# Decay tables ahead of the third piece of w_out, and the fifth tile's scores, mask and exit in another place

## The chip, the cores and the metric

The kernel runs on one core of a Trainium2 chip. The metric is the device time of one execution in microseconds (us); the figures given for the kernel before are a median of three runs. The profile is one further execution, recorded instruction by instruction. TensorE does the matrix products, VectorE and ScalarE the elementwise work and the copies out of PSUM, GpSimd a little elementwise work and the issue of nearly all loads, and SyncE issues stores and the transposing DMAs.

## The reference, cut to what matters

```
# q, k, v: (4 batches, 8 heads, 768 positions, 64), f32
state = gamma[h] * state + k_t (outer) v_t        # gamma[h] = 1 - 2**(-5-h)
y_t   = q_t @ state / sqrt(64)                    # for each of 768 positions
x = y, heads side by side                         # (3072 tokens, 512)
h = x @ w_in                                      # w_in: 512 x 2048
g = h + sin(alpha*h)**2 / (alpha + 1e-9)
out = g @ w_out                                   # w_out: 2048 x 512, out f32
```

## The kernel before

The recurrence is computed in chunks of 128 positions. A tile is one chunk of one batch with all eight heads, and there are 24 tiles. `order` (also `P`) puts the first chunks of the four batches in front, `P[0]` to `P[3]`, which need no state; then come chunks 1 to 5 of batch 0, `P[4]` to `P[8]`, then those of the other batches. The "fifth tile" is `P[4]`, the "sixth" is `P[5]`.

Each tile's q and k are transposed ("turned": `stage_T` on TensorE with a copy out of PSUM, or `turn`, a transposing DMA from SyncE), scores are formed in PSUM tile `pa` (`scores`), multiplied by a 0/1 mask on VectorE (the "mask" step, L349), and the values, scaled by `scale_v` (L156), are summed with them. `burst(old, new)` issues on TensorE what is left of tile `old`, with the scores of tile `new` in between, and returns four closures to be run later. These are `keep` (new state into `s_f`, L446), `hand` (its bf16 copy `s_q`, L452), `mask` (of tile `new`), and `exit` (`leave`, L433 or L436: the tile's result times the decay table `qg[:, c]` goes to `xT`, the input of the second part). With `apart=True` the result lies in two separate PSUM banks and the exit is two instructions. `decay_table(c)` (L229) makes the table for chunk index c on GpSimd, one 128x512 f32 product; five are made.

The second part is the two products with w_in and w_out. `Slot` computes 128 of the 2048 hidden columns for a group of tiles: matmuls L481, the sine on ScalarE L484, the square on ScalarE (L489) or on VectorE (L491, two inputs in SBUF), and the sum on VectorE (`add`, L496), which writes `gT` and frees the slot's PSUM bank. `ff_out` (L506) multiplies `gT` with w_out into `po`. Group 0 has four tiles, the other ten have two each. `F(ts, fs)` issues the w_out products of group 0's tiles `ts` for columns `fs`. When it reaches column 15 it also copies the result out (`take`: L520 on ScalarE for tile 0, L518 on VectorE for tile 1) and SyncE stores it. `fill(n)` issues the next n of the remaining w_out products of tiles 2 and 3. What is left of them after the bursts goes to `phase(1)`. Phases 1 to 10 are alike: slots of one group between products of the group before and a burst at two places.

Every queue is in program order: the schedule is written out by hand, each engine executes its instructions as they are issued in the text and waits at each for its inputs and its buffer. PSUM tags: `mm` has four banks, `pa` and `two` one tile of two banks each. In `two` lie in turn group 0's first two results (`both`) and the `py` of each burst from the sixth tile on.

GpSimd issues the loads in the order of the text: four pieces each of w_in and w_out, in between the first q, k, v tiles. `load_w_in(i, h)` loads columns 4i to 4i+3 in two halves, `load_w_out(i)` the rows for columns 4i to 4i+3 ("third piece" is i = 2). Slot f needs piece f // 4 of w_in, and the product of column f needs piece f // 4 of w_out. GpSimd also scales v of the fifth tile (`scale_v(P[4], nc.gpsimd)`), VectorE that of the sixth.

Of the kernel before, what the change touches and what calls it, by code (L numbers as in the profile page):

```python
# [16 lines left out]
def kernel(  # L17
# [15 lines left out]
    nc = tc.nc  # L33
    B, H, S, D = q.shape
    C = 128
    NCH = S // C
# [33 lines left out]
    def half(x):  # L70
        return slice(64 * x, 64 * x + 64)
# [6 lines left out]
    def spread(j):  # L78

        return j in order[8:11]  # L80

    def chunk_of(t, j):
        b, c = divmod(j, NCH)
        return t[b, :, c * C:(c + 1) * C, :].rearrange("h s d -> s h d")

    def load_chunk(j, names="qkv"):
        for name, src in (("q", q), ("k", k), ("v", v)):
            if name not in names:
                continue
            if name == "v":  # L90
                t = big.tile([128, H, D], BF16, name="vr", tag="vr", bufs=11)
            else:
                if ("qk", j) not in raw:
                    raw["qk", j] = big.tile([128, 2, H, D], BF16, name="qkr", tag="qkr", bufs=9)
                t = raw["qk", j][:, "qk".index(name)]
            if name != "v" and spread(j):
                for o in range(2):
                    nc.gpsimd.dma_start(out=t[:, NP * o:NP * o + NP], in_=chunk_of(src, j)[:, o::2])
            else:
                nc.gpsimd.dma_start(out=t, in_=chunk_of(src, j))  # L100
            raw[name, j] = t

    def wide(j):
        return j >= NCH + 3 and j % NCH > 0
# [24 lines left out]
    def load_w_in(i, h=None):  # L129
        c = slice(i * fw, (i + 1) * fw) if h is None else slice(i * fw + h * fw // 2, i * fw + (h + 1) * fw // 2)  # L130
        nc.gpsimd.dma_start(out=w_in[:, :, c], in_=w_in_v[:, :, c])

    def load_w_out(i, h=None):
        c = slice(i * fo, (i + 1) * fo) if h is None else slice(i * fo + h * fo // 2, i * fo + (h + 1) * fo // 2)
        nc.gpsimd.dma_start(out=w_out[:, c, :], in_=w_out_v[:, c, :])
# [16 lines left out]
    def scale_v(j, eng):  # L152
        t, by = raw["v", j], kg
        if wide(j):
            t, by = t.rearrange("i f p d -> i (f p) d"), kgq
        eng.tensor_mul(t, t, by[:, j % NCH, :, None].to_broadcast([128, H, D]))  # L156
# [71 lines left out]
    def decay_table(c):  # L228
        nc.gpsimd.tensor_mul(qg[:, c], qg[:, 0], step[:, c, :, None].to_broadcast([128, NP, C]))  # L229
# [27 lines left out]
    def stage_T(j, eng=None, tag="two"):  # L257
        pt = psum.tile([128, 2 * NP, 128], BF16, name="pt", tag=tag, bufs=4 if tag == "mm" else 1)
        st["qkT", j] = work.tile([128, 2 * NP, 128], BF16, name="qkT", tag="qkT", bufs=6)
        for i in range(2):  # L260
            for p in range(NP):
                for e in range(2):
                    h = 4 * (p % 2) + 2 * e + p // 2
                    nc.tensor.transpose(pt[half(e), i * NP + p, :], raw["qk"[i], j][:, h, :], ident)
        if eng is nc.scalar:
            nc.scalar.copy(st["qkT", j], pt)
        else:
            nc.vector.tensor_copy(st["qkT", j], pt)
# [70 lines left out]
    def scores(j):  # L339

        qkT = st["qkT", j]
        pa = st["pa", j] = psum.tile([128, 2, 512], F32, name="pa", tag="pa")
        if not wide(j):
            for p in range(NP):
                for f, e in tiles4:
                    nc.tensor.matmul(pa[half(f), e, 128 * p:128 * p + 128], qkT[half(e), NP + p, half(f)],  # L346
                                     qkT[half(e), p, :], start=(p == 0), stop=True, skip_group_check=True)
            aT = st["aT", j] = work.tile([128, 2, NP, 128], BF16, name="aT", tag="aT", bufs=2)
            return {"mask": lambda: nc.vector.tensor_mul(aT.rearrange("p e n t -> p (e n) t"),  # L349
                                                         pa.rearrange("p e (n t) -> p (e n) t", n=NP), mask_bc)}  # L350
        for m in range(2):
            for b, e in tiles4:
                nc.tensor.matmul(pa[half(b), e, 192 * m:192 * m + 128].rearrange("p (f i) -> p f i", f=2),
                                 qkT[half(e), 2 + m, half(b)], qkT[half(e), m:m + 5:4, half(b)],
                                 start=(m == 0), stop=True, skip_group_check=True)
            for b, e in tiles4:
                nc.tensor.matmul(pa[half(b), e, 192 * m + 128:192 * m + 192],
                                 qkT[half(e), 6 + m, half(b)], qkT[half(e), 4 + m, half(b)],
                                 start=False, stop=True, skip_group_check=True)
        aT = st["aT", j] = work.tile([128, 2, 2, 192], BF16, name="aTw", tag="aT", bufs=2)  # L360
        return {"mask": lambda: nc.vector.tensor_mul(aT, pa[:, :, 0:384].rearrange("p e (m t) -> p e m t", m=2),  # L361
                                                     maskq[:, None, None, :].to_broadcast([128, 2, 2, 192]))}
# [96 lines left out]
    def run(more, *kinds):  # L459
        for kind in kinds:  # L460
            if more and kind in more:
                more.pop(kind)()
# [40 lines left out]
    def ff_out(g, ts, f):  # L503
        if (g, ts) not in po:
            po[g, ts] = psum.tile([128, d_model], F32, name="po", tag="mm", bufs=4)
        nc.tensor.matmul(po[g, ts], gT[g][:, f, ts * C:(ts + 1) * C], w_out[:, f, :],  # L506
                         start=(f == 0), stop=(f == FF - 1))
        if f == FF - 1 and (g, ts) not in ((0, 0), (0, 1)):
            take(g, ts)

    def take(g, ts):
        o_sb = work.tile([128, d_model], F32, name="o_sb", tag="o_sb", bufs=3)
        if (g, ts) == end:
            h = d_model // 2
            nc.vector.tensor_copy(o_sb[:, :h], po[g, ts][:, :h])
            nc.scalar.copy(o_sb[:, h:], po[g, ts][:, h:])
        elif g > 0 or ts == 1:
            nc.vector.tensor_copy(o_sb, po[g, ts])  # L518
        else:
            nc.scalar.copy(o_sb, po[g, ts])  # L520
        nc.sync.dma_start(out=out_view[:, groups[g][ts], :], in_=o_sb)
# [75 lines left out]
        scale_v(j, nc.vector)  # L597
    for h in range(2):
        load_w_in(2, h)
    decay_table(1)  # L600
    decay_table(2)
    load_w_out(2)
    for h in range(2):
        load_w_in(3, h)
    decay_table(3)
    decay_table(4)
    load_chunk(order[4], "qk")
    load_w_out(3)
    decay_table(5)
    load_chunk(order[4], "v")  # L610
    for j in order[5:7]:
        load_chunk(j)
# [29 lines left out]
    P = order  # L642
    n3, n4 = 3 * C, 4 * C
    def F(ts, fs):
        for f in fs:
            for t in ts:
                ff_out(0, t, f)
        if FF - 1 in fs:
            for t in ts:
                take(0, t)  # L650

    def early(f, tag="mm"):
        return Slot(0, f, (0, n3), tag=tag)
# [3 lines left out]
    def fill(n):  # L657
        for _ in range(n):
            outs.pop(0)()

    fourth = psum.tile([128, 2, 512], BF16, name="fourth", tag="two", padded_shape=[128, 2, 1024])
    a = early(0).sq("A")
    b = early(1).sq("A")
    half_T(e3, 0, nc.vector, fourth[:, 0])
    c = early(2).sq("A")
# [14 lines left out]
    a = Slot(0, 0, (n3, n4), 4, "pa")  # L680
    F((0, 1, 2), (3,))
    a.sq("D").add()
    a = Slot(0, 4).sq("A")
    for f in range(5, FF):
# [6 lines left out]
        a = b  # L691
# [3 lines left out]
            first_state(e0)  # L695
        if f == 13:
            stage_T(P[4], nc.vector, "pa")
    F((0, 1), (13,))
    scale_v(P[4], nc.gpsimd)
    m4 = scores(P[4])["mask"]  # L700
    m4()
    fill(3)
    stage_T(P[5], nc.scalar, "mm")
    fill(1)
    a.add()
    scale_v(P[5], nc.vector)
    fresh = burst(P[4], P[5], apart=True)
    run(fresh, "keep", "hand", "mask", "exit")
    F((0, 1), (14,))
    F((0, 1), (15,))  # L710


    load_chunk(P[7])
# [3 lines left out]
    load_chunk(P[8], "v")  # L717
    scale_v(P[7], nc.gpsimd)
    load_chunk(P[10], "qk")
    load_chunk(P[9], "v")  # L720
    scale_v(P[8], nc.gpsimd)
    load_chunk(P[10], "v")
# [83 lines left out]
```

## Time and profile before

| | |
|---|---|
| time, median of 3 runs | 212.26 us (212.02 to 212.61) |
| time of the profiled execution | 212.17 us |
| its span, first to last instruction | 210.3 us |
| TensorE busy | 202.7 us (96%) |
| VectorE busy | 156.6 us (74%) |
| ScalarE busy | 154.9 us (74%) |
| GpSimd busy | 117.2 us (56%) |
| granted TensorE clock | 0.998 |

The profiled execution's own time is 1.87 us more than its span: what lies before the first and after the last instruction. A timeline row gives start, duration, engine, source line, operation, output and input tiles, and count; a bracket at its end gives the time that the engine sat idle before the row and what ended that. A duration is from start to end, and consecutive rows of one engine may overlap by some hundredths, as pipelined instructions do.

### The profile page before, as it was taken

The numbers are of one execution on the slowest core, as the hardware profiler recorded it, in microseconds if no ns is written. First come the engines' busy times: TensorE is split into PE (matmuls) and PEld (weight loads), VectorE is DVE, ScalarE is ACT, GpSimd is POOL, SyncE is SP. The second block draws the span as 40 slices with busy tenths as digits, with TensorE's granted clock in tenths as the row PEclk, the third lists the DMA queues.
The fourth block names the chain that finished last, engine by engine and source line by source line (L and its number), as shares of the span: only waits on it lengthen the run. The fifth ranks groups of instructions, "written<-read, shape, count | busy, mean of one in ns | idle before, by whom it ended". The sixth has DMA issues, their size and how long they took to land.

```text
span 210.3 us, 5890 instructions
## 1 busy us (share of the span) xinstructions
PE 202.7 (96%) x2418; PEld 129.9 (62%) x2418; DVE 156.6 (74%) x326; ACT 154.9 (74%) x325; POOL 117.2 (56%) x157
## 2 busy tenths in 40 slices
PE   7899889999999999999999999999999999999994
PEld 3445434456777666666666666766666766666653
DVE  5788998877888987777777777767768768666540
ACT  7778767556998877877777787786786787788821
POOL 8999976799989999998399901002022020000000
PEclk9999999999999999999999999999999999999999
DMA  9999999999999999999999996412412110110112
GB/s 130 152 177 198 201 198 183 154 162 172 155 123 169 121 178 165 170 119 169 177 83 180 148 141 64 103 48 55 101 49 54 53 51 5 50 53 0 50 53 100
DMA packets 102027, 24.78 MB, mean 118 GB/s; under 512 B 93024, under 2 KB 99056, under 8 KB 102000
## 3 DMA queue, kind: packets, MB, share of 16 engines
q0 software_dynamic: 79248, 13.38, 90.6%
q1 hardware_dynamic: 22608, 10.96, 25.6%
q8 instruction: 19, 0.31, 0.6%
q14 instruction: 8, 0.07, 0.1%
q10 hardware_dynamic: 144, 0.07, 0.1%
HBM read 27.27 MB, written 6.29 MB: 160 GB/s over the span
## 4 chain that ended last, share of the span: by engine, by line
PE 84%; DVE 7%; POOL 2%; DMA 2%; ACT 1%; issue 1%; POOLq 0%; DVEq 0%; ACTq 0%
PE ph L481 37%; PE po L506 36%; PE py L336 2%; DMA qkr<-in_k_dram 2%; DVE gT L496 2%; PE poh L531 2%; DVE s L491 2%; PE py L386 1%; POOL qkr L100 1%; DVE aT L286 1%; DVE aT L349 1%; PE pa L346 1%; ACT s L484 1%; POOL vr L100 1%; PE py L395 1%
## 5 line engine op out<-in xcount | busy, mean ns | idle before, releaser
L496 DVE SCALAR_TENSOR_TENSOR gT<-s,rec_alpha,ph 128x256 bf16<-128x256 f32 (+3 forms) x180 | 81.9, 495 | 35.1 <-ACT s L489 34.7
L484 ACT ACTIVATE s<-ph,alpha_sb 128x256 f32<-128x256 f32 (+3 forms) x180 | 78.5, 484 | 35.5 <-PE ph L481 35.3
L481 PE MATMUL ph<-xT,w_in 128*128 128x256 bf16 (+3 forms) x720 | 98.9, 280 | 0.7 <-DVE gT L496 0.6
L506 PE MATMUL po<-w_out,gT 128*128 128x512 bf16 x368 | 95.4, 380 | 0.8 <-DVE gT L496 0.7
L481 PEld LDWEIGHTS <-w_in 128*128 128x128 bf16 x720 | 69.6, 98 | 31.8 <-issue 1.6
L489 ACT ACTIVATE s<-s 128x512 f32<-128x512 f32 (+1 forms) x91 | 56.9, 625 | 2.9
L506 PEld LDWEIGHTS <-gT 128*128 128x128 bf16 x368 | 33.8, 98 | 27.2 <-DVE gT L496 1.5
L452 POOL CAST s_q<-s_f 128x256 bf16<-128x256 f32 x5 | 2.0, 396 | 44.3 <-DVE s_f L446 25.7
L120 POOL DMA_DIRECT2D qk_seq<-in_q_dram x24 | 17.0, 793 | 3.9 <-DMA v_seq<-in_v_dram 3.9
L518 DVE COPY o_sb<-po 128x512 f32<-128x512 f32 x20 | 13.8, 691 | 5.2 <-PE po L506 5.2
L120 POOL DMA_DIRECT2D qk_seq<-in_k_dram x24 | 16.9, 757 | 0.9 <-DMA qk_seq<-in_q_dram 0.7
L120 POOL DMA_DIRECT2D v_seq<-in_v_dram x24 | 16.9, 773 | 0.0
L156 POOL TENSOR_TENSOR v_seq<-v_seq,kgq 128x512 bf16<-128x512 bf16 x13 | 13.7, 1074 | 5.0 <-DMA v_seq<-in_v_dram 5.0
L433 DVE TENSOR_TENSOR xT<-py,qg 128x512 bf16<-128x512 f32 x19 | 13.0, 685 | 1.1 <-PE py L402 1.1
L361 DVE TENSOR_TENSOR aTw<-pa,maskq 128x768 bf16<-128x768 f32 x13 | 12.4, 953 | 0.0
L100 POOL DMA_DIRECT2D vr<-in_v_dram x11 | 10.3, 932 | 0.7 <-DMA w_in<-in_moe_w_in_dram 0.5
L551 PE MATMUL spare<-warm 128*128 128x512 bf16 x25 | 8.4, 459 | 1.2 <-DVE warm L176 1.2
L349 DVE TENSOR_TENSOR aT<-pa,mask 128x1024 bf16<-128x1024 f32 x7 | 8.5, 1219 | 0.4 <-PE pa L346 0.4
L452 ACT CAST s_q<-s_f 128x256 bf16<-128x256 f32 x14 | 5.5, 391 | 3.6 <-DVE s_f L446 3.2
L156 POOL TENSOR_TENSOR vr<-vr,kg 128x512 bf16<-128x512 bf16 x5 | 5.5, 1105 | 3.1 <-DMA vr<-in_v_dram 3.1
L100 POOL DMA_DIRECT2D qkr<-in_k_dram x7 | 6.2, 893 | 1.1 <-DMA w_out<-in_moe_w_out_dram 1.1
L336 PE MATMUL py<-qkT,s_q 64*64 64x128 bf16 x160 | 6.4, 228 | 0.4 <-DVE o_sb L518 0.3
(99 smaller groups left out, 159.6 us busy)
## 6 DMA issues: line engine op xcount, KB each, us to landing
out_dram<-o_sb SPq DMA_DIRECT2D x23, 256.0 KB, 2.6
w_in<-in_moe_w_in_dram POOLq DMA_DIRECT2D x6, 256.0 KB, 11.4
w_out<-in_moe_w_out_dram POOLq DMA_DIRECT2D x3, 512.0 KB, 11.4
vr<-in_v_dram POOLq DMA_DIRECT2D x11, 128.0 KB, 6.3
qk_seq<-in_q_dram POOLq DMA_DIRECT2D x16, 80.0 KB, 6.7
qk_seq<-in_k_dram POOLq DMA_DIRECT2D x16, 80.0 KB, 4.9
v_seq<-in_v_dram POOLq DMA_DIRECT2D x16, 80.0 KB, 4.9
qkr<-in_q_dram POOLq DMA_DIRECT2D x7, 128.0 KB, 5.5
```

The source lines that it names most:

```text
L100: nc.gpsimd.dma_start(out=t, in_=chunk_of(src, j))
L120: nc.gpsimd.dma_start(out=o, in_=src[bt, head(b, m, e), cs[0] * C:, :].rearrange("(f i) d -> i f d", i=64))
L156: eng.tensor_mul(t, t, by[:, j % NCH, :, None].to_broadcast([128, H, D]))
L336: last = nc.tensor.matmul(o, s[half(e), 2 * b + m, :], to, start=(m == 0), stop=True, skip_group_check=True)
L361: return {"mask": lambda: nc.vector.tensor_mul(aT, pa[:, :, 0:384].rearrange("p e (m t) -> p e m t", m=2), maskq[:, None, None, :].to_broa ...
L433: nc.vector.tensor_mul(o, st["pyw", old][:, :, 0:256].rearrange("p b (m t) -> p b m t", m=2), by)
L481: nc.tensor.matmul(self.ph[:, m, :], w_in[:, i, f * 128:(f + 1) * 128], xT[g][:, i, self.lo:self.hi], start=(m == 0 and i == 0), stop=(i = ...
L484: nc.scalar.activation(out=self.s[:, m, :], in_=self.ph[:, m, :], func=ACTF.Sin, scale=alpha_sb[:, f:f + 1])
L489: nc.scalar.activation(out=self.s, in_=self.s, func=ACTF.Square)
L496: nc.vector.scalar_tensor_tensor(gT[self.g][:, f, self.lo:self.hi], self.s[:, m, :], rec_alpha[:, f:f + 1], self.ph[:, m, :], op0=ALU.mult ...
L506: nc.tensor.matmul(po[g, ts], gT[g][:, f, ts * C:(ts + 1) * C], w_out[:, f, :], start=(f == 0), stop=(f == FF - 1))
L518: nc.vector.tensor_copy(o_sb, po[g, ts])
```

## The change

Tables 1 to 4 are made one after the other ahead of the load of w_out's third piece; before, two of them stood behind the last piece of w_in. Table 5 moves from its place behind the last piece of w_out into the loads of phase 1, behind q and k of `P[10]`. The scores of `P[4]` are issued ahead of the column-13 products; the turn of `P[5]` then comes after one filling product instead of three, and the last slot's `add` comes ahead of the mask on VectorE. Five filling products instead of four stand ahead of the burst, so one fewer is left for phase 1. The fifth tile's exit runs behind the two `F` lines, and so on VectorE behind the copy of tile 1 of group 0.

```diff
     for h in range(2):
         load_w_in(2, h)
-    decay_table(1)
-    decay_table(2)
+    for c in range(1, NCH - 1):
+        decay_table(c)
     load_w_out(2)
     for h in range(2):
         load_w_in(3, h)
-    decay_table(3)
-    decay_table(4)
     load_chunk(order[4], "qk")
     load_w_out(3)
-    decay_table(5)
     load_chunk(order[4], "v")
     for j in order[5:7]:
         load_chunk(j)
...
-    F((0, 1), (13,))
     scale_v(P[4], nc.gpsimd)
     m4 = scores(P[4])["mask"]
+    F((0, 1), (13,))
+    fill(1)
+    stage_T(P[5], nc.scalar, "mm")
+    a.add()
     m4()
-    fill(3)
-    stage_T(P[5], nc.scalar, "mm")
-    fill(1)
-    a.add()
+    fill(4)
     scale_v(P[5], nc.vector)
     fresh = burst(P[4], P[5], apart=True)
-    run(fresh, "keep", "hand", "mask", "exit")
+    run(fresh, "keep", "hand", "mask")
     F((0, 1), (14,))
     F((0, 1), (15,))
+    run(fresh, "exit")
...
     load_chunk(P[10], "qk")
+    decay_table(NCH - 1)
     load_chunk(P[9], "v")
     scale_v(P[8], nc.gpsimd)
     load_chunk(P[10], "v")
```

## The prediction

> **What bounds the kernel now.** I read the page first, then the busy times by stretch, the chain that ended last, and the timeline of each engine where TensorE stood still.
>
> ```profile
> span 210.3 us, 5890 instructions
> sum 150.00, PE 149.93 PEld 102.21 DVE 112.81 ACT 118.75 POOL 72.83; mean PE 29.99 PEld 20.44 DVE 22.56 ACT 23.75 POOL 14.57
> ```
>
> The second row sums five stretches that cover 50 to 200 us: TensorE is busy in 149.93 of 150 us. From 50 us on the kernel is a fixed amount of TensorE work, so a change ahead of that moves the end by as much as TensorE enters this part earlier, and by the matmuls that it is spared there. The losses lie before. The chain crosses VectorE:
>
> ```profile
> 23.08 1.41 DVE s L491
> 24.52 1.78 DVE gT L496 x5
> 26.30 1.82 DVE s L491
> 28.95 0.82 PE po L506 x3
> 29.77 0.86 PE ph L481 x4
> ...
> 22.36 2.75 PE L481 MATMUL ph<-xT,w_in 128*128 128x512 bf16 x12
> 25.69 1.02 PE L481 MATMUL ph<-xT,w_in 128*128 128x512 bf16 x4 [0.58 <-DVE gT L496]
> ```
>
> Two squares on VectorE (L491) take 1.41 and 1.82 us, and TensorE waits behind them for `gT`. The next fence groups all squares, and all decay tables, as minimum/median/maximum in ns; below it are the rows of GpSimd and the other engines from that time.
>
> ```profile
> L491 DVE TENSOR_TENSOR s<-s x6: 681/684/1893, 23.1 to 37.8; 128x512 f32<-128x512 f32 x6
> L229 POOL TENSOR_TENSOR qg<-qg,step x5: 1034/1081/1472, 16.8 to 26.5; 128x512 f32<-128x512 f32 x5
> ...
> 15.15 1.54 POOL L131 DMA_DIRECT2D w_in<-in_moe_w_in_dram x2
> 16.76 2.04 POOL L229 TENSOR_TENSOR qg<-qg,step 128x512 f32<-128x512 f32 x2
> 18.75 0.82 POOL L135 DMA_DIRECT2D w_out<-in_moe_w_out_dram x1
> 19.56 1.49 POOL L131 DMA_DIRECT2D w_in<-in_moe_w_in_dram x2
> 21.05 2.88 POOL L229 TENSOR_TENSOR qg<-qg,step 128x512 f32<-128x512 f32 x2
> 26.47 1.08 POOL L229 TENSOR_TENSOR qg<-qg,step 128x512 f32<-128x512 f32 x1
> ...
> 20.54 2.49 DVE L156 TENSOR_TENSOR vr<-vr,kg 128x512 bf16<-128x512 bf16 x2
> ...
> 24.68 1.25 ACT L484 ACTIVATE s<-ph,alpha_sb 128x512 f32<-128x512 f32 x2
> ```
>
> A square alone takes 0.684. The long ones run while GpSimd makes tables 4 (until 23.93) and 5 (26.47 to 27.55), and both end 0.55 us behind the table (24.49 and 28.12). The two products L156 beside tables 3 and 4 take 2.49 instead of the 1.37 that two operations of their size, like the square, would. Tables 1 and 2 hold nobody up and take 1.02 each: VectorE's work there reads one input from PSUM.
>
> **Step 1: tables 3 and 4 go to 18.75, table 5 leaves.** Four tables at 1.02 end at 16.76 + 4.08 = 20.84. Table 4 then overlaps the first L156 (20.54) by 0.3 us; the price is 0 to 0.55 (the tail seen above). I take 0.3: the pair ends at 20.54 + 1.37 + 0.3 = 22.2, hidden, since the next square starts no earlier than now (I leave it at 23.08: it waits for its sines). It then ends at 23.76, not 24.49. Of the five sums at 24.52 (1.78) the last, slot 4's, is a full one of about 0.74 (a row of this form stands below, at 41.83); the four small ones, 1.04 in all, end near 24.8 and free the `pa` bank, and slot 4's ends near 25.55. Slot 5's square waits for no sine (24.68 + 0.69 = 25.37), runs 25.57 to 26.25, and its sum ends at 27.04, not 28.90.
>
> On TensorE: one matmul takes 0.86 / 4 = 0.215 (the row at 29.77). The 12 matmuls from 22.36 end at 24.95, and slot 7 follows without its wait: 25.69 to 24.95. From slot 7 to the column-5 products lie 4 + 3 + 4 = 11 matmuls, 2.37 us, where the rows have 28.95 - 25.69 = 3.26. So these start at 27.32, not 28.95, with `gT` ready since 27.04. **The gain at this place is 1.62 us**, all of the two waits.
>
> **Step 2: what is late next, the loads.** Moved past: w_out's third piece and w_in's fourth, issued two tables later (2.05 us by the bare price, 2.94 at 1.472 each). What follows goes out sooner: the fifth tile's q at 20.84 + 0.82 + 1.49 = 23.15 instead of 23.93, and what stands behind table 5's old place by one more table, until an issue has to wait for an earlier transfer to land, as the row at 30.43 does. The rows of the DMA issues end in the time to landing.
>
> ```profile
> w_in<-in_moe_w_in_dram POOLq DMA_DIRECT2D x1, 256.0 KB, 11.1
> w_out<-in_moe_w_out_dram POOLq DMA_DIRECT2D x1, 512.0 KB, 11.4
> w_in<-in_moe_w_in_dram POOLq DMA_DIRECT2D x1, 256.0 KB, 11.9
> ...
> 30.43 0.88 POOL L100 DMA_DIRECT2D qkr<-in_k_dram  x1 [1.14 <-DMA w_out<-in_moe_w_out_dram]
> ...
> qkr<-in_k_dram POOLq DMA_DIRECT2D x1, 128.0 KB, 9.6
> ```
>
> In this order: w_in's third piece, first half, issued 15.15, lands 26.25; w_out's third, issued 18.75, lands 30.15; w_in's fourth, first half, issued 19.56, lands 31.5; the sixth tile's k, issued 30.43 once w_out's third has landed, lands 40.0. At 20.84, then, transfers issued at 15.15 are still 5.4 us from landing: the queue does not run dry, and the pieces issued later still have their turn behind the same bytes. I take a slip of 0, with 0 to 2.9 as bounds. Slot 8 needs w_in's third piece at 24.95 + 7 x 0.215 = 26.46, just after 26.25.
>
> Between w_in's fourth piece and that k stand the fifth tile's loads and w_out's fourth piece; a slip there is the same slip at k, so k is the one to count. It is the load that TensorE overtakes:
>
> ```profile
> 39.26 1.03 PE L506 MATMUL po<-w_out,gT 128*128 128x512 bf16 x4
> 41.32 0.64 PE L264 MATMUL pt<-ident,qkr 128*64 128x128 bf16 x16
> 42.62 0.30 PE L336 MATMUL py<-qkT,s_q 64*64 64x128 bf16 x7 [0.17 <-DVE gT L496]
> 43.58 1.47 PE L506 MATMUL po<-w_out,gT 128*128 128x512 bf16 x6
> 46.63 0.31 PE L336 MATMUL py<-qkT,s_q 64*64 64x128 bf16 x8 [0.25 <-DVE o_sb L518]
> 48.41 1.03 PE L481 MATMUL ph<-xT,w_in 128*128 128x256 bf16 x8
> ...
> 40.69 1.23 DVE L349 TENSOR_TENSOR aT<-pa,mask 128x1024 bf16<-128x1024 f32 x1 [0.39 <-PE pa L346]
> 41.83 0.74 DVE L496 SCALAR_TENSOR_TENSOR gT<-s,rec_alpha,ph 128x512 bf16<-128x512 f32 x1
> 45.23 0.75 DVE L436 TENSOR_TENSOR xT<-py,qg 128x256 bf16<-128x256 f32 x2
> 45.89 0.68 DVE L518 COPY o_sb<-po 128x512 f32<-128x512 f32 x1
> ```
>
> The four matmuls at 39.26 come at 37.64. The turn of the sixth tile stands two matmuls sooner, so at 41.32 - 1.62 - 0.43 = 39.27; its second half, k, would begin near 39.55 and waits to 40.05. It ends near 40.33. Queued behind this new wait on TensorE are four filling matmuls and the burst; nothing else fills it.
>
> **Step 3: add ahead of mask, exit behind the copies.** Now the burst reaches its second bank at 42.62 only when the last slot's sum (41.83 to 42.57) has freed it, as that stood behind the mask. Turned round, the sum ends near 40.0 and the mask near 41.1, both before the burst, which starts at 40.33 + 4 x 0.215 + 0.1 = 41.3. It took 43.58 - 42.62 = 0.96 and ends near 42.26 instead of 43.58: 1.32 earlier, one filling matmul (0.215) more done.
>
> Then 46.63 waits for the `two` bank, which tile 1's copy frees on VectorE, now behind the two exits (together 0.75, about 0.66 net of overlap). With the exits behind it, the bank is free 0.66 sooner, and TensorE's own work is the limit: 9 matmuls, a turn of 0.64 and about 0.2 of changes of tile, 2.77 where 3.05 passes now, 0.28 saved. ScalarE's copy of the seventh tile's turn, moved with TensorE, may hold the scores behind it and take back some of this; I take 0.2 (bounds 0 and 0.28). Its exit is now late behind the copy, but its readers, phase 1's slots, wait for the sixth tile's exit in any case. So 48.41 becomes 46.9, 1.52 earlier, and phase 1 has one matmul less: 1.52 + 0.215, rounded 1.75.
>
> **Step 4: table 5 in phase 1.** It costs GpSimd 1.03 to 1.47 behind q and k of `P[10]`; queued behind it are v of `P[9]`, the scaling of `P[8]`'s v, and all later loads.
>
> ```profile
> 55.30 1.04 POOL L156 TENSOR_TENSOR vr<-vr,kg 128x512 bf16<-128x512 bf16 x1 [0.51 <-DMA vr<-in_v_dram]
> 63.76 0.31 PE L336 MATMUL py<-qkT,s_q 64*64 64x128 bf16 x8
> ```
>
> This scaling waits 0.51 for its data anyway, so it ends some 0.5 to 1 us later, by 57.4; its reader is the burst at 63.76, which comes near 62. Table 5's own reader is `P[8]`'s exit behind that burst. VectorE has no two-input SBUF operation left there that table 5 could stretch. I price it at 0, covered by over 4 us.
>
> **Sum.** Against the profiled execution: 212.17 - 1.75 = 210.4 (span near 208.55). The median of the runs shown is 0.09 above that execution, so measured medians near 210.4 to 210.5. An outcome within 0.3%, 0.64 us, is what a measurement of this kernel can hardly tell from no change.
>
> **The rivals.** *A: the late pieces slip (slower).* If the load queue did run dry between 18.75 and 20.84, w_out's third piece and everything behind it, the sixth tile's k too, would land later by all of the added delay, and as TensorE stands at that k, each us costs one: with 2.05 the time is 212.45, no change; with 2.94, tables at the stretched 1.472, 213.3, slower. It decides from a slip of 1.75 on, and is slower by over 0.3% from 2.4. For it: the two pieces are moved past two tables. Against: the 5.4 us of backlog at 20.84. [...] Chance 0.07.
>
> *B: the ninth tile's turn holds the fourth burst.* `P[8]` is turned by a DMA from SyncE:
>
> ```profile
> 49.63 0.33 SPq L521 DMA_DIRECT2D out_dram<-o_sb  x1
> 50.16 10.75 SPq L273 DMA_TRANSPOSE qkT<-qkr  x3
> ...
> qkT<-qkr SPq DMA_TRANSPOSE x1, 6.9
> ...
> 57.80 0.23 PE L346 MATMUL pa<-qkT 64*64 64x128 bf16 x2
> ```
>
> It lands at 50.16 + 6.9 = 57.06, and its scores at 57.80 would come at 56.05. If the turn does not come sooner, 1.0 of the 1.75 is lost: 211.4. Against: it stands on SyncE behind the store at 49.63, whose copy comes sooner, as the tenth filling product, which completes tile 2, now stands ahead of the second burst. Chance 0.13.
>
> *C: the long squares are not the tables' doing.* Then only the end of step 3 is left, 0.2 + 0.215: 211.75, no change that can be told. Against it are two squares in six stretched, both beside a table. Chance 0.07.
>
> **How the numbers follow.** The forecast gets 0.68, and 0.05 is left for what I do not see. The forecast's own range: 209.9 if k lands 0.5 sooner and TensorE does not stand, 211.0 with a slip of 0.6. To hold 8 in 10 it reaches to B: 209.9 to 211.5. Faster by over 0.3% (below 211.5): the forecast and nearly all of B, 0.83; within: C and half of A, 0.1; slower: the other half of A and most of what I do not see, 0.07.
>
> **What would show it.** Step 1: all six squares near 0.68, four tables at about 1.02 from 16.8, slot 7 without a wait, column-5 products near 27.3. Step 2: w_in's fourth piece lands near 31.5 though issued near 21.7, and TensorE waits for k at the turn near 40. Step 3: second burst near 45 without a wait for L518, phase 1's first slot near 46.9. Wrong it would be if a slot waits for w_in's fourth piece, if L156 is stretched beyond the square's start at 23.08, or if TensorE shows gaps behind 50 us.

## The result and the profile after

| | before | after |
|---|---|---|
| time, median of 5 runs | 212.26 us | 211.12 us (210.75 to 211.37) |
| ratio, 95% interval | | 0.9945 (0.9928 to 0.9962) |
| profiled execution, time and span | 212.17, 210.3 us | 211.37, 209.6 us |

The change makes the kernel faster by 0.55%, 1.14 us. The forecast was 1.75 to 1.8, so about two thirds of it came. Where the prediction said that VectorE's squares would no longer be stretched, the groups (minimum/median/maximum in ns) and VectorE's timeline of the changed kernel say:

```profile
L491 DVE TENSOR_TENSOR s<-s x6: 680/684/692, 24.1 to 37.2; 128x512 f32<-128x512 f32 x6
L229 POOL TENSOR_TENSOR qg<-qg,step x5: 1033/1034/1090, 17.5 to 54.4; 128x512 f32<-128x512 f32 x5
...
20.99 1.72 DVE L156 TENSOR_TENSOR vr<-vr,kg 128x512 bf16<-128x512 bf16 x2
24.10 0.69 DVE L491 TENSOR_TENSOR s<-s 128x512 f32<-128x512 f32 x1 [1.40 <-ACT s L484]
```

All six squares are at 0.68, the tables at their bare price, and the L156 pair takes 1.72 instead of the 1.29 that e6 below shows for it. That is hidden, as VectorE then waits 1.40 for the sines. TensorE's and GpSimd's timeline, with the landing of the two transfers that the second step turned on:

```profile
20.74 0.41 PE L312 MATMUL pye<-aT,vr 128*64 128x128 bf16 x8 [0.59 <-DMA vr<-in_v_dram]
23.37 3.66 PE L481 MATMUL ph<-xT,w_in 128*128 128x512 bf16 x16
29.03 1.03 PE L481 MATMUL ph<-xT,w_in 128*128 128x512 bf16 x4
40.31 0.90 PE L264 MATMUL pt<-ident,qkr 128*64 128x128 bf16 x16
45.69 0.31 PE L336 MATMUL py<-qkT,s_q 64*64 64x128 bf16 x8
47.57 1.03 PE L481 MATMUL ph<-xT,w_in 128*128 128x256 bf16 x8
...
17.53 4.03 POOL L229 TENSOR_TENSOR qg<-qg,step 128x512 f32<-128x512 f32 x4
21.51 0.81 POOL L135 DMA_DIRECT2D w_out<-in_moe_w_out_dram  x1
31.27 0.87 POOL L100 DMA_DIRECT2D qkr<-in_k_dram  x1 [1.68 <-DMA w_out<-in_moe_w_out_dram]
...
w_out<-in_moe_w_out_dram POOLq DMA_DIRECT2D x1, 512.0 KB, 9.5
qkr<-in_k_dram POOLq DMA_DIRECT2D x1, 128.0 KB, 9.5
```

Slots 4 to 7 are one row of 16 matmuls without a gap, and from slot 4 to slot 9 it takes 29.03 - 23.37 = 5.66 us, which is 26 matmuls at 0.215 and nothing else. Before it took 29.60 - 22.36 = 7.24 (the row for slot 9 is in the next fence). But slot 4 starts 1.01 later than in the profile before, although nothing ahead of it was changed: TensorE waited 0.59 for the fourth tile's v, at a place where the first profile had no wait (and 0.29 ahead of that for the same tile's q, at 16.48). Two rows of the profile before:

```profile
19.63 0.41 PE L312 MATMUL pye<-aT,vr 128*64 128x128 bf16 x8
...
29.60 1.03 PE L481 MATMUL ph<-xT,w_in 128*128 128x512 bf16 x4
```

The turn of the sixth tile takes 0.90 instead of 0.64: the wait for k, 0.26. The second burst starts without its wait for the copy, and phase 1 starts at 47.57, not at 48.41. The last copy of the kernel then loses some of it again. Its rows, before and after:

```profile
207.34 0.29 DVE L537 COPY o_sb<-poh 128x128 f32<-128x128 f32 x1 [2.84 <-PE poh L531]
...
206.64 0.29 DVE L537 COPY o_sb<-poh 128x128 f32<-128x128 f32 x1 [3.19 <-DMA out_dram<-o_sb]
```

Before, this copy waited for TensorE. After, it waited for an earlier store to give a buffer back, 0.35 longer (3.19 against 2.84).

So the theory to test was that of the prediction: the tables stretch VectorE's operations, the moved pieces do not slip, the rest comes from the burst. Two rivals stood against it for the missing 0.6 us: that the change itself makes loads late, or that the profile before was an odd one, in which the stretched squares cost more than they usually do. The medians below leave out the slower runs of e4 (three) and e6 (one), and for e7_later, where four of five runs had a granted clock of 0.99, the profiled execution at 1.0 stands in.

### The profile page after: what moved, and what is told of

Its sections match the earlier page's. It is cut to its first block, busy times and chain, and to the rows that moved or that the text cites. A ratio compares the mean times of both kernels' runs of the same rounds, so it can differ in the third digit from the quotient of the medians.

```text
span 209.6 us, 5890 instructions
## 1 busy us (share of the span) xinstructions
PE 202.2 (96%) x2418; PEld 129.5 (62%) x2418; DVE 154.0 (73%) x326; ACT 155.0 (74%) x325; POOL 116.3 (55%) x157
## 4 chain that ended last, share of the span: by engine, by line
PE 77%; DMA 14%; POOL 6%; DVE 1%; issue 1%; DVEq 0%; POOLq 0%
PE po L506 35%; PE ph L481 33%; DMA qkr<-in_k_dram 5%; DMA w_out<-in_moe_w_out_dram 5%; DMA w_in<-in_moe_w_in_dram 3%; PE py L336 2%; POOL qg L229 2%; POOL qkr L100 2%; DMA out_dram<-o_sb 1%; PE py L386 1%; POOL vr L100 1%; POOL w_in L131 1%; PE pa L346 1%; PE py L395 1%; PE pt L264 1%; PE pa L353 1%
## 5 line engine op out<-in xcount | busy, mean ns | idle before, releaser
L496 DVE SCALAR_TENSOR_TENSOR gT<-s,rec_alpha,ph 128x256 bf16<-128x256 f32 (+3 forms) x180 | 81.9, 495 | 35.4 <-ACT s L489 35.1
L156 POOL TENSOR_TENSOR v_seq<-v_seq,kgq 128x512 bf16<-128x512 bf16 x13 | 13.5, 1062 | 3.7 <-DMA v_seq<-in_v_dram 3.7
L100 POOL DMA_DIRECT2D qkr<-in_q_dram x7 | 6.4, 910 | 0.9 <-DMA w_in<-in_moe_w_in_dram 0.9
L156 POOL TENSOR_TENSOR vr<-vr,kg 128x512 bf16<-128x512 bf16 x5 | 5.5, 1106 | 2.3 <-DMA vr<-in_v_dram 2.3
```

What stands on the lines that cost most here:

```text
L496: nc.vector.scalar_tensor_tensor(gT[self.g][:, f, self.lo:self.hi], self.s[:, m, :], rec_alpha[:, f:f + 1], self.ph[:, m, :], op0=ALU.mult ...
```

## Experiments

All ratios are to the kernel before, run on the same chip. Its median was 212.70 us beside e1 to e4, 212.77 beside b_again, e5, e6 and t1, and 212.46 beside e7, t2 and t3, so ratios are to be compared, not medians across these groups. "Slot 4 to 9" is the time from the row of the 12 or 16 matmuls to slot 9's row; 5.65 is without any wait.

| run | median, us | ratio (95%) | slot 4 starts | slot 4 to 9 | phase 1 starts |
|---|---|---|---|---|---|
| before, first profile | 212.26 | | 22.36 | 7.24 | 48.41 |
| b_again (before) | 212.52 | 0.998 (0.9951 to 1.0009) | 23.13 | 6.60 | 48.54 |
| after, first profile | 211.12 | 0.9945 (0.9928 to 0.9962) | 23.37 | 5.66 | 47.57 |
| e3_again (after) | 211.36 | 0.9927 (0.99 to 0.9954) | 23.39 | 5.65 | 47.63 |
| e1_tables | 212.23 | 0.9975 (0.9957 to 0.9993) | 23.54 | 5.65 | 48.00 |
| e5_table5 | 211.95 | 0.9957 (0.9933 to 0.998) | 23.53 | 5.76 | 48.09 |
| e2_order | 212.09 | 0.9971 (0.9947 to 0.9996) | 23.26 | 6.65 | 48.43 |

**The two halves of the change.** e1 is the move of the tables alone.

> Only the decay tables move (1 to 4 ahead of w_out's third piece, 5 into phase 1); the burst's text is as before. If the stretched squares are the tables' doing, all six squares take 0.68 us, the column-5 products start 1.5 to 1.7 us sooner counted from the start of the 12 matmuls ahead of them, and the time falls by 1.0 to 1.5 us (some of 1.6 is lost at the sixth tile's k). If the squares are stretched by something else, they stay above 1.3 us and the time falls by less than 0.3 us.

```diff
 (kernel before)
-    decay_table(1)
-    decay_table(2)
+    for c in range(1, NCH - 1):
+        decay_table(c)
     load_w_out(2)
...
-    decay_table(3)
-    decay_table(4)
...
-    decay_table(5)
...
     load_chunk(P[10], "qk")
+    decay_table(NCH - 1)
```

All squares were at 0.68 to 0.69 and the wait-free 5.65 us came, so the stretched squares are the tables' doing. The time fell by only 0.47 us, under the 1.0 to 1.5 expected. The profile shows one place where this execution gave some back, rival B of the prediction, with the ninth tile's turn landing 8.1 us after its issue at 49.76:

```profile
57.12 0.31 PE L336 MATMUL py<-qkT,s_q 64*64 64x128 bf16 x8
57.87 0.42 PE L346 MATMUL pa<-qkT 64*64 64x128 bf16 x16 [0.27 <-DMA qkT<-qkr]
```

In undisturbed bursts the scores follow 0.27 behind the burst's first row (57.53 and 57.80 before); here it is 0.75, so 0.48 is lost.

e2 is the order around the burst alone, with the tables where they were.

> Only the order around the first burst changes; the tables stay where they were. If the prediction's third step is right, the time falls by 0.3 to 0.5 us: the second burst starts without a wait for the copy L518, and phase 1 has one matmul less. The rival, that the two parts only pay together or that the turn of the sixth tile now stands at the loads, gives 0 to 0.2.

```diff
 (kernel before; the second hunk of the change, nothing else)
-    F((0, 1), (13,))
     scale_v(P[4], nc.gpsimd)
     m4 = scores(P[4])["mask"]
+    F((0, 1), (13,))
...
-    run(fresh, "keep", "hand", "mask", "exit")
+    run(fresh, "keep", "hand", "mask")
     F((0, 1), (14,))
     F((0, 1), (15,))
+    run(fresh, "exit")
```

The time fell by 0.6 us at the middle, a little above the forecast (the interval reaches from 0.1 to 1.1), and the second burst had no wait. In the profile slot 9 to phase 1 takes 18.52 us, where both profiles of before have 18.81 (48.41 - 29.60 in the first): 0.29, and with the matmul that phase 1 is spared 0.5. The two halves add up: 0.25% and 0.29% make 0.54%, beside 0.55% and 0.73% for the whole in its two measurements; the intervals are too wide to say more.

**Which profile was the odd one?** e3 is the changed kernel once more, b_again the kernel before once more.

> The changed kernel once more, for a second profile. If the shortfall of the first profile came from w_in's first piece landing 1.4 us late by chance (6.6 after its issue, 5.2 in the kernel before), it lands some 5.2 after its issue here and the profiled execution takes 210.3 to 210.8. If the shortfall is the change's own (late pieces, the wait for k), the profiled execution takes 211.2 or more with w_in's first piece on time.

> The kernel before once more, for a second profile. In the first one w_in's first piece landed 5.2 us after its issue; in the five profiles of other kernels taken since, which are the same up to there, 6.1 to 6.7. If the first profile was the odd one, it lands 6.1 or more here, the 12 matmuls start near 23.3 instead of 22.36, and the column-5 products start at 29.2 to 29.4, only 0.3 later than in the first, as the stretched squares swallow 0.6 of the 0.9. If late landings come with the change, it lands at 5.2 again.

In e3, w_in's first piece landed 6.7 after its issue, late again, and the profiled execution took 211.76: neither of the two outcomes, so it decides nothing by itself. In b_again it landed at 5.6, under the 6.1 expected, but the fourth tile's v was late all the same, and slot 4 started at 23.13. So w_in's first piece was the wrong sign to go by (in e7_later it landed at 5.1, and slot 4 still started at 23.18), and a late start does not come with the change. Of the fourteen profiles the first of before has the earliest start; only e6 (22.61) and t2 (22.65) come near, and the others lie from 22.98 to 23.54. TensorE's and VectorE's rows of b_again:

```profile
20.50 0.41 PE L312 MATMUL pye<-aT,vr 128*64 128x128 bf16 x8 [0.63 <-DMA vr<-in_v_dram]
23.13 2.75 PE L481 MATMUL ph<-xT,w_in 128*128 128x512 bf16 x12
26.11 1.02 PE L481 MATMUL ph<-xT,w_in 128*128 128x512 bf16 x4 [0.23 <-DVE gT L496]
29.07 0.82 PE L506 MATMUL po<-w_out,gT 128*128 128x512 bf16 x3 [0.43 <-DVE gT L496]
29.73 1.03 PE L481 MATMUL ph<-xT,w_in 128*128 128x512 bf16 x4
48.54 1.03 PE L481 MATMUL ph<-xT,w_in 128*128 128x256 bf16 x8
...
20.71 3.58 DVE L156 TENSOR_TENSOR vr<-vr,kg 128x512 bf16<-128x512 bf16 x2
24.22 0.68 DVE L491 TENSOR_TENSOR s<-s 128x512 f32<-128x512 f32 x1
26.63 1.61 DVE L491 TENSOR_TENSOR s<-s 128x512 f32<-128x512 f32 x1
```

Slot 4 starts 0.77 later than in the first profile, but the column-5 products only 0.12 later (29.07 against 28.95). Tables 3 and 4 now fall on the L156 pair, which takes 3.58 and still ends at 24.29, and the square behind it is not stretched; only the one beside table 5 is. The two waits are 0.23 and 0.43 instead of 0.58 and 0.72. A late start is swallowed by the waits that the tables cause, so removing the waits saves less when the start is late: 6.60 - 5.65 = 0.95.

The other profiles bear this out. From slot 4's start to phase 1 the kernel before takes 26.05 us in its first profile and 25.41 in b_again, less when it starts later. The changed kernel takes 24.20 (after), 24.24 (e3) and 24.25 (t1) with starts at 23.37, 23.39 and 22.98, and 24.38 (t2) with 22.65: with the waits gone, an earlier start is passed on nearly whole. The two executions of before, 0.77 us apart at slot 4, end 0.15 us apart (212.17 and 212.32), which fits this. For the kernel before it rests on these two profiles.

**Table 5 alone.** e5 moves only table 5 out of the way.

> The kernel before with table 5 alone moved into phase 1; tables 3 and 4 stay. Theory: with w_in's first piece late, only the square beside table 5 was long (1.89 us; the one beside table 4 0.80), so this alone takes all squares to under 0.9 and gives nearly all of what the tables' move gives: the column-5 products 0.8 to 1.0 us sooner counted from the 12 matmuls, and a time like that of the tables' move alone, 0.3 to 0.6 us under the kernel before. Rival: tables 3 and 4 carry half of it, and this gives under 0.2 us.

```diff
 (kernel before)
     load_w_out(3)
-    decay_table(5)
     load_chunk(order[4], "v")
...
     load_chunk(P[10], "qk")
+    decay_table(NCH - 1)
```

```profile
21.15 2.46 DVE L156 TENSOR_TENSOR vr<-vr,kg 128x512 bf16<-128x512 bf16 x2
24.26 0.79 DVE L491 TENSOR_TENSOR s<-s 128x512 f32<-128x512 f32 x1 [0.65 <-ACT s L484]
26.79 0.68 DVE L491 TENSOR_TENSOR s<-s 128x512 f32<-128x512 f32 x1
```

All squares stayed under 0.9, and the column-5 products came 5.11 us after slot 4's start instead of the 5.94 of b_again, 0.83 sooner, as forecast. The median fell by 0.8 us, more than the 0.3 to 0.6 forecast and no less than e1's 0.47, but the intervals of e1 and e5 overlap. With loads as late as here, tables 3 and 4 cost 0.11 us where they stood (slot 4 to 9 took 5.76, without any wait 5.65).

**Reads or any GpSimd work?** e6 puts other GpSimd work in the tables' old places.

> The kernel before with tables 3, 4 and 5 made in phase 1, and in their old places GpSimd runs iota twice for each, which writes a scratch tile of the table's size and reads nothing from memory. If the tables stretch VectorE's squares because both read, the squares are 0.68 here and the column-5 products come as early after the 12 matmuls as in the changed kernel (5.0 us). If any GpSimd instruction that writes memory does it, one square stays above 1.2 us.

```diff
 (kernel before; stand_in() runs iota twice into a 128x512 f32 scratch tile)
-    decay_table(3)
-    decay_table(4)
+    for _ in range(2):
+        stand_in()
...
-    decay_table(5)
+    stand_in()
...
     load_chunk(P[10], "qk")
+    for c in range(3, NCH):
+        decay_table(c)
```

```profile
20.56 1.29 DVE L156 TENSOR_TENSOR vr<-vr,kg 128x512 bf16<-128x512 bf16 x2
21.06 0.62 POOL L234 IOTA scratch<- 128x512 f32 x1
...
L497 DVE TENSOR_TENSOR s<-s x6: 681/684/693, 23.3 to 36.5; 128x512 f32<-128x512 f32 x6
...
56.39 1.03 PE L487 MATMUL ph<-xT,w_in 128*128 128x256 bf16 x8 [1.00 <-DVE gT L502]
```

Lines stand six lower in this kernel (L497 is the square). With iotas beside them, neither the pair nor a square was stretched, and slot 4 to 9 took 5.65: GpSimd work that only writes does not hold VectorE up, and of the two theories the tables' reading is left. An iota differs from the product in more than its reading, and no other stand-in was run. The kernel's time, 213.08 us (1.0019, 0.9995 to 1.0043), says nothing on this: with three tables in phase 1, table 3 came too late, VectorE's exit of the seventh tile waited 2.01 for it, and TensorE lost 1.00 at 56.39 behind VectorE:

```profile
54.87 0.69 DVE L439 TENSOR_TENSOR xT<-py,qg 128x512 bf16<-128x512 f32 x1 [2.01 <-POOL qg L229]
```

So table 5 fits into phase 1, but table 3 does not.

**Do the moved pieces slip?** Six and twelve iotas ahead of w_out's third piece in the changed kernel delay it further.

> The changed kernel with six iotas on GpSimd (about 0.62 us each, reading nothing) ahead of w_out's third piece, which so goes out 3.8 us later still, near 25.3. Theory of the backlog: the load queue still holds work then, the pieces land where they did (w_out's third near 31, the sixth tile's k near 40.8), and TensorE's first phase-1 slot starts within 0.2 us of 47.6. Rival A of the prediction, a slip with the issue: k lands 3.8 us later and the time rises by 3 to 4 us.

> As the run before with twelve iotas: w_out's third piece goes out 7.7 us later than in the changed kernel, near 29.2, after w_in's third piece has landed (28 to 28.7). The queue is empty then by the theory of the backlog too: w_out's third piece lands at 34 or later, k slips by 3 us or more, and the time rises by 2.5 to 4 us. If the time stays within 0.5 us of the changed kernel, the loads do not hold TensorE there at all.

```diff
 (kernel after; e7_late: range(6), e7_later: range(12), one iota each)
     for c in range(1, NCH - 1):
         decay_table(c)
+    for _ in range(6):
+        stand_in()
     load_w_out(2)
```

| | e2_order | after | e7_late | e7_later |
|---|---|---|---|---|
| w_out's third piece issued | 19.41 | 21.51 | 25.21 | 28.39 |
| ... lands | 30.9 | 31.0 | 32.1 | 34.2 |
| time, us | 212.09 | 211.12 | 212.73 | 215.37 |
| ratio to before | 0.9971 | 0.9945 | 1.0004 (0.9981 to 1.0027) | 1.014 (one execution) |

An issue 2.1 us later moved the landing by 0.1 (w_in's fourth piece, 20.23 and 22.31, landed at 32.2 and 32.3): the queue did hold enough work, and rival A is out for the change. A further 3.7 us moves it by 1.1, and TensorE's wait for k at the turn shows it. I had expected no slip and phase 1 within 0.2 us of 47.6; it starts at 48.89, and the whole gain of the change is gone, though not the 3 to 4 us of rival A. The turn in e7_late, and a slot in e7_later:

```profile
42.12 0.41 PE L269 MATMUL pt<-ident,qkr 128*64 128x128 bf16 x8 [0.56 <-DMA qkr<-in_k_dram]
...
36.59 1.04 PE L486 MATMUL ph<-xT,w_in 128*128 128x512 bf16 x4 [1.77 <-DMA w_in<-in_moe_w_in_dram]
```

With the issue at 28.39 the slots themselves wait, 1.77 for w_in at 36.59, and the execution takes 4.0 us more than the profiled one of the changed kernel (215.37 and 211.37). So the loads start to slip somewhere between the change's delay and 3.7 us more; where is not shown.

**The tail and the loads behind.** t1 is the changed kernel with `bufs=4` instead of 3 for `o_sb`; t2 also issues `load_chunk(P[7])` ahead of the scaling of the fifth tile's v on GpSimd; t3 also puts the sixth tile's q and k ahead of the fifth tile's v; e4 is that last edit alone on the changed kernel.

> The changed kernel with four buffers instead of three for the output copies. In both profiles of the changed kernel the last copy (L537) waited for a store to land, 0.36 and 0.65 us after TensorE was done. If that is a loss of the tail, the wait goes and the time falls by 0.3 to 0.6 us against the changed kernel. If the stores themselves set the end, the end moves by less than 0.1 us.

> The changed kernel with the sixth tile's q and k loaded ahead of the fifth tile's v. If TensorE is held at the turn by k, k lands some 0.8 us sooner, the wait at the turn goes (0.26 to 0.5 us), the fifth tile's v is scaled 0.8 to 1.7 us later and still in time, and the time falls by 0.2 to 0.5 us against the changed kernel. If v takes the place of k as the late load, the time stays the same or rises.

> The changed kernel with four output buffers, and with the eighth tile's loads issued ahead of the scaling of the fifth tile's v, in GpSimd's idle 2.3 us. Expected: the ninth tile's keys and its turn land up to 2 us sooner, so that its scores have no wait in any run; the profile shows no change up to there, and the time stays within 0.3 us of the kernel with four buffers (210.7 to 211.0), with less spread. If the fifth tile's scaled v then comes late for the first burst (scaling ends after 41.9), the time rises.

> As the run before, with the sixth tile's q and k ahead of the fifth tile's v. The wait at the sixth tile's turn (0.3 us) goes, and with the eighth tile's loads already out the ninth tile's turn is not late, as it was where the keys alone were put first. Expected 0.2 to 0.4 us under the kernel with four buffers. Rival: the fifth tile's scaled v is late for the first burst, and nothing is gained.

```diff
 (t1: kernel after)
-        ... tag="o_sb", bufs=3)
+        ... tag="o_sb", bufs=4)
 (t2: t1 and)
+    load_chunk(P[7])
     scale_v(P[4], nc.gpsimd)
 (e4: kernel after and; t3: t2 and)
-    load_chunk(order[4], "v")
-    for j in order[5:7]:
-        load_chunk(j)
+    load_chunk(order[5], "qk")
+    load_chunk(order[4], "v")
+    load_chunk(order[5], "v")
+    load_chunk(order[6])
```

| run | median, us | ratio (95%) |
|---|---|---|
| t1_four_out | 210.84 | 0.9911 (0.9878 to 0.9945) |
| t2_seventh_first | 210.74 | 0.9926 (0.9902 to 0.995) |
| t3_both | 210.81 | 0.9932 (0.9906 to 0.9958) |
| e4_keys_first | 211.83 | 0.9973 (0.994 to 1.0006) |

The last copies of t1, e4's scores of the ninth tile, and t3's first burst:

```profile
205.95 0.29 DVE L537 COPY o_sb<-poh 128x128 f32<-128x128 f32 x1 [2.84 <-PE poh L531]
...
57.27 0.42 PE L346 MATMUL pa<-qkT 64*64 64x128 bf16 x16 [0.60 <-DMA qkT<-qkr]
...
42.45 0.30 PE L395 MATMUL py<-aT,vr 64*64 64x128 bf16 x8 [0.32 <-POOL vr L156]
```

In t1 the tail's wait is gone, as expected, and its ratio is the lowest of all. But its interval overlaps that of the changed kernel, so the loss of the tail is shown in the profile and not in the times. t2 and t3 are no faster than t1, and t2's ninth turn landed no sooner (49.29 + 6.0, against 50.05 + 5.3 in t1). e4 is a miss: k is in time (the turn takes 0.64), but the fifth tile's v lands later, GpSimd stands 4.29 us at its scaling instead of 2.32, all that is behind goes out later, and TensorE waits 0.60 for the ninth tile. Its time was not lower than the changed kernel's; that it was higher is not shown, as the intervals overlap. With the eighth tile's loads put ahead, t3 moved the wait to the scaled v (0.32). The wait for k can be shifted about, but the loads ahead of 42 us come one behind the other.

## Why the prediction was right or wrong

Right were the direction and the range (measured 211.12 in 209.9 to 211.5), and the mechanism of all four steps; the size of step 1 was wrong. That the time lies in the range is partly luck: the forecast's own range ended at 211.0, and the part up to 211.5 was added for rival B, which the two profiles of the changed kernel do not show.

**Step 1, mechanism right, size wrong.** The squares and both waits did what was said: 5.66 us against the 5.6 of bare matmuls. The term of 1.62 us was mis-sized: against the first profile it came (7.24 - 5.66 = 1.58), but against a kernel before with a start as late as b_again's it is 0.95 (6.60 - 5.65). The working took both waits from one profile in which the fourth tile's v was in time, and treated 23.08 as the place where VectorE's chain always starts. It did not ask what a start 0.8 later would do: the waits take most of it up.

**Step 2, right on the landing and on the place of the new wait.** No slip (0.1 us for 2.1 us of delay), and TensorE stood at the sixth tile's k, for 0.26 instead of 0.5, as both it and the load came later.

**Step 3, right.** The second burst had no wait for the copy, and alone the step gave 0.5 us by the profile (0.6 by the medians) where 0.42 was forecast. Phase 1 started at 47.57, not at 46.9, because slot 4 started 1.01 later; counted from slot 4 it came sooner than forecast (24.20 against 46.9 - 22.36 = 24.54).

**Step 4, right.** Table 5 at 54.44 held nobody up in the changed kernel.

**Rival B.** It did not come about in the two profiles of the changed kernel, but my reason against it was wrong. I expected the ninth tile's turn to be issued sooner, as the store ahead of it comes sooner. The store did, but the turn then waited for the ninth tile's k, whose last load was issued near 44.8 and took 5.3 us. It was issued at 50.15, as before, and landed in 5.5 us instead of 6.9, and why it was shorter is not shown:

```profile
50.15 10.55 SPq L273 DMA_TRANSPOSE qkT<-qkr  x3
...
qkT<-qkr SPq DMA_TRANSPOSE x1, 5.5
...
56.74 0.23 PE L346 MATMUL pa<-qkT 64*64 64x128 bf16 x2
```

Landing at 55.65, it was 1.1 ahead of its scores; with the 8.1 of e1 it would have been 1.5 behind.

**What the sum lacked.** The tail: with three buffers the last copy waited for a store in eight of eleven profiles, 0.2 to 0.65 us, in both of the changed kernel and in neither of the kernel before. That this comes with the change is not shown, as e1, e2, e5 and others waited too; the store took 2.6 and 2.7 us in the two profiles of before, and 3.0, 3.3 and 3.1 in after, e3 and e1.

By the two profiles with a late start, b_again and after: slot 4 is 0.24 later, slot 4 to 9 0.94 shorter, phase 1 0.97 earlier with one matmul (0.215) less, the last matmuls 1.19 earlier (203.74 and 202.55), and the last copy 0.83 earlier, as the store takes back 0.35.

## What to carry to other kernels

A wait read from one profile is worth what it is worth at that profile's timing: ask whether an upstream load that comes a microsecond later would fill the same gap, and take a second profile of the kernel before if the gap stands behind loads. GpSimd arithmetic that reads SBUF is best put where VectorE works out of PSUM. An issue can be moved later at no cost while the queue ahead of it holds enough work: here 2.1 us cost 0.1, and 3.7 us more cost 1.1. When the middle of a kernel gets faster by a microsecond, look at the tail and at the next just-in-time load: both took back some tenths here.

## What the runs showed of the hardware

A GpSimd product with two operands in SBUF held up VectorE operations with two inputs in SBUF until about 0.55 us behind its own end, up to 3.58 us for a pair that takes 1.29 (b_again). In other profiles the product was held up too: 1.47 us in the first of before and 1.52 in e2 and e5, instead of 1.03. VectorE operations with an input in PSUM were not held up (in the changed kernel two sums of L496 took 1.13 beside a table, as they did before with none beside them), and GpSimd's iota, which writes as much and reads nothing, held up none (a median of 0.684 for the six squares). The Trainium skill, page "SBUF — State Buffer", section "SBUF: two separate sides", says that VectorE operations with two SBUF inputs contend only with GpSimd operations that read SBUF; the run with iotas agrees with it. The same section's rule on descriptors, that GpSimd cannot write those of its loads while VectorE runs an operation in a two-port mode, is not about L156: it is a tensor_tensor, which by that section has no such mode. The trace fits: the issue at 21.51, beside the L156 pair, took 0.81, as others did.

I had not expected that loads issued in the same order at the same time would land so differently: w_in's first piece took 5.1 to 6.8 us over the profiles. The turn of the ninth tile took 4.6 to 8.1, though not from the same time of issue.
